# Linear attention followed by a gated convolution unit: another order of steps, other PSUM banks, and copies moved between engines

## The chip, the cores and the metric

The kernel runs on one core of a Trainium2 chip. The metric is the device time of one execution in microseconds (us), lower is better. Five engines work side by side, each through its own queue in order: TensorE (PE in the profile; its weight loads are PEld), VectorE (DVE), ScalarE (ACT), GpSimd (POOL) and SyncE (SP), which here only issues DMAs. GpSimd issues the loads of inputs in the same queue as its arithmetic.

## The reference

Inputs are float32. `q`, `k`, `v` have the shape (8 batches, 8 heads, 576 positions, 64), `w_phi` is 64 x 128, and the second part has two 512 x 512 weights and five taps for each of 512 channels.

```python
def phi(x):                                   # features of q and of k
    proj = x @ w_phi                          # [..., 576, 128]
    proj = proj - max(abs(proj), axis=-1)
    return concat([exp(proj), exp(-proj)])    # 256 features
kv  = sum over s of phi(k)[s, f] * v[s, d]
z   = sum over s of phi(k)[s, f]
att = (phi(q) @ kv) / (phi(q) @ z + 1e-6)     # [8, 8, 576, 64]
x   = att, heads side by side                 # [8, 576, 512]
gate = sigmoid(sum over t of conv_w[t] * x shifted down by 4 - t)
out  = (gate * (x @ w_val)) @ w_out           # [8, 576, 512]
```

## The kernel before

**Units and quads.** The 576 positions of a head are laid out as 128 partitions of nine half-blocks. The first eight half-blocks of a head make one unit; the ninth ones of the eight heads of two batches make another. So each of the four groups of two batches has nine units, 36 in all (numbers 0 to 35). Two heads form a quad (0 to 15), of which two make a batch (0 to 7).

**Tokens.** Everything that the kernel does is one of 1200 tokens in the string `ORDER`. A loop at the end of the kernel runs through them and calls the function of each, with its number, its PSUM banks (behind `@`) and its engine (behind `:`; `D` VectorE, `A` ScalarE, `P` GpSimd):

```python
    with tc.manual_schedule():
        for token in ORDER.split():
            head, _, eng = token.partition(":")
            head, _, bank = head.partition("@")
            ...
            ops[name](*args)
```

The order in the string is therefore the order of instructions in every engine's queue; no scheduler changes it. Waits between engines follow from the tiles that the instructions share. PSUM has eight banks of 128 x 512 float32, and the list names the bank of each product.

**The tokens that matter here,** with the number of their unit, quad, batch or output:
- `LK`, `LQ`, `LW`, `LC`: the first loads, on SP's and ScalarE's queues (LW the weights of phi, LC the five taps). `LD0` to `LD28`: the other loads, on GpSimd's queue (L331; LD27 is `w_val`, L336; LD28 is `w_out` in eight issues, L342).
- `CK`, `CQ`, `W2`: first casts of k, q and of the weights of phi (L254, L257, L260). `ND`: the negative identity (L251). `FL`: matmuls whose result nothing reads (L346).
- `T`: transposes of k and q of a unit on TensorE (L365, L370), `Tc` copies them out of PSUM (L245 on VectorE and GpSimd, L243 on ScalarE). From unit 24 on, but for unit 29, `TK` and `TQ` do this by a DMA transpose on SP's queue (L376).
- `PK`, `PQA`: products with the weights of phi, positions on the partitions (L393). `mK`, `mKb`, `mQ`, `mQa`: maxima of absolute values on VectorE (L411). `K0` to `K3`: exponentials for k on ScalarE (L460). `E`: factors exp of the maxima (L454). `V`: v times these factors, in GpSimd's or VectorE's queue: one 128 x 1024 product (L495) and a small cast (L500).
- `PQ` (L549), `SH` (the maximum taken off by matmuls, L557), `Qa` and `Q` (L580, two exponentials each): features of q.
- `KVa`, `KVb`: phi(k) times v (L523); `CA`, `CB` copy the result out of PSUM into the tile KVS. `NUM` (L622): numerator and denominator, three for a quad; `XN` divides (L628, L631).
- `XP`: transpose of a quad's result into the tile XT, by TensorE (L645, copied by `XC`) up to number 15, by a DMA on SP's queue (L641) from 16 on. `XQ` and `XD`: the same for the ninth half-blocks (L654). `HL`: the halo, the last four columns copied to the front shifted by one position (L245).
- `GA`: the convolution of a batch as matmuls with diagonal matrices (L692), `TH` its tanh on ScalarE (L702). `VAa`, `VAb`: two matmuls each of `x @ w_val` (L707). `GV`: gate times value on VectorE (L723). `OUT`: the output product, four matmuls (L732), `OE` takes it out of PSUM with a factor 0.5 (L739 on ScalarE, L741 on VectorE), `ST` stores it by SP's queue, `SU` by ScalarE's. Tokens ending in `t` (`GAt`, `THt`, `GVt`, `OUTt`, `OEt`, `STt`) do this for the ninth half-blocks of a group.
- `TP`, `CW`, `DG`, `DH`: the taps transposed and spread into diagonal matrices. `WS`: `w_val` into its final order.

The engine of a copying token picks the instruction:

```python
    def copy(eng, dst, x):
        if eng == "A":
            nc.scalar.activation(dst, x, AF.Copy)
        else:
            engines[eng].tensor_copy(dst, x)
```

Tiles rotate: six T tiles, four VT tiles, four KVS tiles, three output tiles of two outputs each. A token that writes one waits until the readers of the tile that it replaces are done.

Of the kernel before, what the change touches and what calls it, by code (L numbers as in the profile page):

```python
# [39 lines left out]
FL20@6 PQA2@0,6 mQa2 mQ2 PQ1@4,3 mQ3 SH1 Qa1 T4@0 Tc4:D T5@1 Tc5:D FL21@2 PK4@4,2 mKb4 Q1 PQA4@5,0  # L40
mQa4 K04 K14 K24 PQ2@6,7 SH2 Qa2 mK4 E4 V4:P PQA5@1,3 mQa5 mQ4 TP0@5 T6@4 Tc6:D PQ3@1,6 PQA6@4,0
K34 CW0 mQ5 SH3 mQa6 mQ6 T7@2 Q2 Qa3 PK5@3,7 KVa0@5,4 KVb0 mKb5 LD10 Q3 Tc7:D CA0:D CB0:D PK6@0,6
mKb6 K05 K15 mK5 T8@1 Tc8:D PQ4@2,5 LD9 K25 NUM0@4 XN0 K06 DG0:P SH4 KVa1@3,1 KVb1 K35 DH0:P K16
Qa4 Q4 PK7@7,4 E5 K07 K17 mK6 E6 CA1:D CB1:A mKb7 PQA7@2,0 mQa7 mQ7 PK8@3,5 K08 NUM1@0 mKb8 NUM3@2
XN1 LD27 K27 K37 PQ5@1,0 NUM2@4 mK7 K18 SH5 XN3 mK8 XN2 V5:P PQA8@7,3 mQa8 K26 mQ8 K28 Qa5 NUM5@2
# [6 lines left out]
Q8 VAa0@0 VAb0 NUM10@6 K012 GV0 K311 K212 XQ2@0 K112 XN10 K312 mK12 PK13@4,7 K013 NUM7@1 K111
XD2:A K113 XP6@3 XC6:A mKb13 K213 XN7 NUM11@6 XN11 PQ9@2,0 SH9 Qa9 mK13 mK11 XP5@1 VAa1@3 VAb1
K313 XC5:D XP4@4 XC4:A E11 Q9 XP7@6 XC7:D XQ3@5 PQ10@1,2 XD3:D HL3:P PQA12@7,6 GV1 HL2:P mQa12
PQA11@5,4 mQa11 SH10 Qa10 mQ12 Q10 E12 T14@3 Tc14:D mQ11 OUT0@7 E13 OE0:D GA1@5,0 V11:P KVa4@3,2
KVb4 PK14@4,7 TH2 VAa7@5 LD15 VAb7 VAa4@6 mKb14 TH3 K014 PQ11@0,1 K114 VAb4 GV7 mK14 LD18 LD16
T15@5 SH11 GV4 PQA13@4,6 K214 Tc15:D CA4:A CB4:A K314 Qa11 Q11 mQa13 PQA14@3,7 NUM12@2 PQ12@5,4
# [6 lines left out]
E16 K316 Tc19:D ST1 K017 K117 K217 VAb9 K317 mK17 GA2@2,5 TH4 PQA18@7,1 LD25 TH5 mQa18 OUT2@4 mQ18
T20@7 Tc20:A OE2:D PQA19@2,1 mQa19 PQ16@3,5 SH16 E17 PQA17@6,4 KVa6@7,2 V15:P V16:P Qa16 Q16 GV9
KVb6 LD22 LD17 mQa17 mQ17 PK18@0,6 mKb18 K018 CA6:A V17:P K218 LD26 T21@3 Tc21:D mQ19 OUT5@4 CB6:D
VAa11@5 VAb11 K118 OE5:A mK18 LD24 PK19@7,3 mKb19 K318 K019 K219 KVa7@1,2 PK20@4,0 mKb20 KVb7 K020
CA7:D K319 GV11 VAa10@6 VAb10 NUM18@1 GV10 CB7:D K120 mK20 PQ17@5,3 SH17 XN18 K119 K220 Qa17
VAa8@6 VAb8 GV8 K320 Q17 OUT4@2 mK19 PQA20@5,4 mQa20 PK21@1,6 K021 mKb21 OE4:A ST5 K221 OUT6@0
OE6:A mQ20 NUM21@7 T22@3 NUM20@5 K321 XN21 Tc22:A PQ18@2,4 XN20 NUM19@0 XN19 SH18 Qa18 XQ6@5 E18  # L70
V18:P XD6:D NUM22@7 XN22 NUM23@6 XN23 PQ19@3,0 XP12@5 XC12:D ST3 T23@7 Tc23:D XP13@2 SH19 TK24
TQ24 TQ25 XC13:D Q18 HL6:D XP14@6 XC14:D XP15@5 XC15:D K121 XQ7@4 XD7:D HL7:P Qa19 Q19 OUT9@7 mK21
PK22@2,3 K022 mKb22 E19 K122 OUT7@6 TK25 OE7:A ST7 OE9:D GA3@0,4 E20 mK22 V19:P TH6 PQA21@7,6
mQa21 VAa13@2 VAb13 E21 mQ21 PQ20@7,1 GV13 SH20 PQA24@0,6 mQa24 TH7 K222 OUTt0@4 mQ24 OEt0:D
VAa12@0 K322 Qa20 Q20 PQA22@5,2 V20:P KVa8@3,6 V21:P KVb8 mQa22 mQ22 E22 V22:P PK23@7,4 mKb23
# [12 lines left out]
XN33 TK32 OUT13@4 K329 OE13:A NUM35@0 mKb30 XN35 XQ10@5 NUM34@7 XN34 K130 mK30 XD10:A K230
PQ27@6,4 SH27 Qa27 E29 V27:P K330 XP22 Q27 XP23 XP20 ST13 V28:P VAa19@5 VAb19 OUT15@0 TK33 mQ30
PK31@7,6 OE15:D V29:P VAa18@2 VAb18 mKb31 XQ11@1 K031 PQ28@3,0 TQ33 SH28 GV19 XD11:A ST15  # L90
KVa12@4,1 GV18 TQ34 K131 K231 Qa28 mK31 PQA29@5,2 K331 KVb12 mQa29 Q28 OUT16@7 CA12:D CB12:A
PK32@3,4 PQA31@5,6 K032 mQ29 mQa31 PQ29@0,2 OE16:A mQ31 TK34 TQ35 SH29 Qa29 Q29 NUM36@1 XN36 K132
OUT17@5 OE17:D mKb32 HL10:P OUT19@7 OE19:D HL11:P K232 GA5@0,5 K332 TH11 mK32 NUM37@2 XN37
# [6 lines left out]
PQA35@1,4 XP26 GAt2@2 K135 HL12:D OUT20@5 mKb35 NUM43@0 HL13:P mQa35 mQ35 THt2 mK35 PQ34@1,4 K235  # L100
K335 OE20:A ST21 E34 SH34 Qa34 E35 NUM42@7 GVt2 XN42 GA6@2,5 ST19 VAa25@7 XN43 VAa24@1 VAb25 TH13
V34:P TH12 GV25 XP28 VAa26@0 VAb26 NUM44@5 XN44 XP29 PQ35@6,2 KVa15@3,7 Q34 V35:P KVb15 CA15:A
SH35 OUT22@4 CB15:D XQ14@5 VAa27@3 VAb27 Qa35 Q35 NUM45@7 VAb24 GV26 XD14:D ST17 HL14:P NUM46@0
# [767 lines left out]
```

## Time and profile before

| | |
|---|---|
| median of 3 runs | 220.04 us (218.84 to 220.24) |
| the profiled execution's own time | 219.92 us |
| its span | 218.1 us |
| TensorE clock granted, mean | 0.988 |
| busy: TensorE, VectorE, ScalarE, GpSimd | 199.3, 184.3, 188.7, 113.4 us |
| HBM read and written | 30.48 MB and 9.44 MB |

The span is what the profile shows; the execution's own time has some 1.8 us more around it. Matmuls are pipelined, so a busy TensorE is not one at its peak. The profile's lines name the source line, the engine, the operation and the tiles (out<-in); in a timeline the first two numbers are the start in us and the time from the first start to the last end, and the bracket at the end tells for how long the engine stood idle just before and what ended that.

### The profile page before, as it was taken

The page shows a single profiled execution, that of the slowest core. Times are in us where ns is not written, and L with a number is a line of the kernel's source. Part 1 is how long each engine was busy: PE and PEld are TensorE (multiplying, and loading weights), DVE is VectorE, ACT ScalarE, POOL GpSimd, SP SyncE. Part 2 cuts the span into 40 slices and gives each one's busy share as a digit, 9 for nine tenths or more (in the row PEclk, how much of TensorE's full clock was granted, in tenths as well). Part 3 has the DMA queues.
Part 4 walks back from the last instruction along what each step waited for, and adds up shares of the span by engine and source line. Part 5 has one row for each costly group of instructions (what it writes and reads, how often), then busy time and mean ns, then how long its engine had stood idle before and what let it go on. Part 6 is the DMA issues. An engine that isn't in the chain of part 4 may idle for free.

```text
span 218.1 us, 9723 instructions
## 1 busy us (share of the span) xinstructions
PE 199.3 (91%) x4171; PEld 133.8 (61%) x4202; DVE 184.3 (84%) x369; ACT 188.7 (87%) x426; POOL 113.4 (52%) x141
## 2 busy tenths in 40 slices
...
GB/s 154 185 208 190 94 164 163 109 109 99 201 19 60 208 99 205 204 128 208 218 227 99 129 162 67 85 8 99 121 126 180 117 118 77 132 150 138 187 177 189
DMA packets 40116, 30.61 MB, mean 140 GB/s; under 512 B 22021, under 2 KB 35205, under 8 KB 40074
## 3 DMA queue, kind: packets, MB, share of 16 engines
...
q10 hardware_dynamic: 624, 0.98, 1.4%
q8 instruction: 32, 0.52, 1.0%
...
HBM read 30.48 MB, written 9.44 MB: 183 GB/s over the span
## 4 chain that ended last, share of the span: by engine, by line
PE 61%; DVE 16%; ACT 9%; DMA 5%; issue 4%; SPq 2%; ACTq 0%; DVEq 0%
PE PS L732 11%; PE PS L707 9%; PE PS L622 7%; PE PS L393 7%; PE PS L523 6%; PE PS L557 5%; DVE MK L411 4%; PE PS L692 4%; ACT KTIL L460 3%; ACT QTIL L580 3%; DVE MQ L411 3%; PE PS L365 3%; DVE XN L631 3%; PE PS L549 3%; DMA OS<-in_k_dram 2%
## 5 line engine op out<-in xcount | busy, mean ns | idle before, releaser
L495 POOL TENSOR_TENSOR VT<-vN,E 128x1024 bf16<-128x1024 bf16 x36 | 68.6, 1907 | 51.0 <-issue 22.3
L460 ACT ACTIVATE KTIL<-PS 128x512 bf16<-128x512 f32 x144 | 84.0, 666 | 2.7 <-PE PS L393 1.9
L580 ACT ACTIVATE QTIL<-PS 128x512 bf16<-128x512 f32 x144 | 79.4, 676 | 1.2 <-PE PS L557 0.8
L411 DVE TENSOR_REDUCE MK<-PS 128x4 f32<-128x512 f32 x72 | 48.2, 683 | 3.7 <-PE PS L393 3.1
L411 DVE TENSOR_REDUCE MQ<-PS 128x4 bf16<-128x512 f32 x72 | 46.9, 683 | 2.3 <-PE PS L393 2.2
L707 PE MATMUL PS<-XT,WVAL 128*128 128x512 bf16 x109 | 31.2, 380 | 1.1 <-issue 0.3
L393 PE MATMUL PS<-W,T 64*128 64x128 bf16 x576 | 28.1, 219 | 3.9 <-DVE MQ L411 0.8
L732 PE MATMUL PS<-WOUT,GV 128*128 128x512 bf16 x116 | 30.7, 380 | 0.7 <-issue 0.2
L631 DVE TENSOR_TENSOR XN<-PS,RCP 128x384 bf16<-128x384 f32 x48 | 26.8, 558 | 1.7
L622 PE MATMUL PS<-KVS,QTIL 128*128 128x65 bf16 (+1 forms) x640 | 26.9, 195 | 1.4 <-DVE MQ L411 1.4
L622 PEld LDWEIGHTS <-QTIL 128*128 128x128 bf16 (+1 forms) x640 | 23.2, 100 | 8.1 <-issue 2.8
L393 PEld LDWEIGHTS <-T 64*128 64x128 bf16 x576 | 17.5, 94 | 16.3 <-issue 9.9
L723 DVE SCALAR_TENSOR_TENSOR GV<-GATE,PS 128x512 bf16<-128x512 bf16 x32 | 21.4, 682 | 4.4 <-ACT GATE L702 3.4
L245 POOL COPY XT<-XT 128x504 bf16<-128x504 bf16 x11 | 6.6, 606 | 35.2 <-DVE XT L245 13.5
L523 PE MATMUL PS<-VT,KTIL 64*128 64x65 bf16 x1152 | 22.2, 192 | 0.5 <-DVE T L245 0.4
L557 PE MATMUL PS<-nident,MQ 128*128 128x128 bf16 x288 | 22.5, 222 | 0.0
L523 PEld LDWEIGHTS <-KTIL 64*128 64x128 bf16 x1152 | 20.6, 96 | 2.1 <-issue 1.0
L557 PEld LDWEIGHTS <-MQ 128*128 128x128 bf16 x288 | 16.8, 99 | 6.9 <-issue 5.9
L732 PEld LDWEIGHTS <-GV 128*128 128x128 bf16 x128 | 11.2, 98 | 11.0
L702 ACT ACTIVATE GATE<-PS 128x1024 bf16<-128x1024 f32 x16 | 15.7, 1024 | 2.2 <-PE PS L692 2.1
L707 PEld LDWEIGHTS <-WVAL 128*128 128x128 bf16 x128 | 10.6, 98 | 10.6 <-issue 1.2
L741 DVE TENSOR_SCALAR OS<-PS 128x512 f32<-128x512 f32 x16 | 11.0, 685 | 5.9 <-PE PS L732 5.8
...
## 6 DMA issues: line engine op xcount, KB each, us to landing
...
kN<-in_k_dram POOLq DMA_DIRECT2D x7, 576.0 KB, 9.0
qN<-in_q_dram POOLq DMA_DIRECT2D x7, 576.0 KB, 5.8
vN<-in_v_dram POOLq DMA_DIRECT2D x7, 576.0 KB, 8.6
...
vN<-in_v_dram POOLq DMA_DIRECT2D x2, 288.0 KB, 11.5
...
```

The costliest lines, as they stand in the source:

```text
L393: nc.tensor.matmul(PS[:, bank[rg], blk * P:(blk + 1) * P], u.T[r, i, blk, :], W2[r, :], start=True, stop=True,)
L411: nc.vector.tensor_reduce(dst, PS[:, bank, :].rearrange("p (b f) -> p b f", f=F), AX.X, ALU.max, apply_absolute_value=True,)
L460: nc.scalar.activation(u.KT[:, ft, rg, :, :].rearrange("p b f -> p (b f)"), PS[:, u.PK[rg], :], AF.Exp, scale=1.0 if ft == 0 else -1.0,)
L495: e.tensor_tensor(u.VT[:, :, :, 0:D], unit_cols(u, "v").unsqueeze(1).to_broadcast([P, 2, 8, D]), E.to_broadcast([P, 2, 8, D]), ALU.mult,)
L523: nc.tensor.matmul(PS[:, m.kv[h2], o:o + E1], u.KT[r, ft, c % 2, c // 2, :], u.VT[r, ft, c, :], start=(j == 0), stop=(j == NJ - 1),)
L557: nc.tensor.matmul(PS[:, u.PQ[rg], blk * P + r.start:blk * P + r.stop], u.MQ[r, rg, blk:blk + 1].to_broadcast([r.stop - r.start, P]), nide ...
L580: nc.scalar.activation(u.QT[:, ft, :, rg, :], PS[:, u.PQ[rg], :].rearrange("p (b t) -> p b t", t=64), AF.Exp, scale=1.0 if ft == 0 else -1.0,)
L622: nc.tensor.matmul(y, f, k, start=(ft == 0), stop=(ft == 1), skip_group_check=True)
L631: nc.vector.tensor_tensor(m.XN[:, 3 * s:3 * s + 3, :].rearrange("p a (x d) -> p (a x) d", d=D), nv[:, :, 0:D], RCP[:, :].unsqueeze(2).to_b ...
L707: nc.tensor.matmul(PS[:, m.val[jt], :], WVAL[:, dt, jt * P:(jt + 1) * P], planes(m, dt, 0), start=(dt == 0), stop=(dt == 3),)
L723: nc.vector.scalar_tensor_tensor(out=m.GV[:, jt, :], in0=m.GATE[jt // 2][:, jt % 2, :], scalar=1.0, in1=PS[:, m.val[jt], :], op0=ALU.add, ...
L732: nc.tensor.matmul(PS[:, bank[0], :], m.GV[:, jt, j * P:(j + 1) * P], WOUT[:, jt, :], start=(jt == 0), stop=(jt == 3),)
```

## The change

Only the string `ORDER` is replaced. Both strings have the same 1200 tokens apart from banks and engines; nearly every token has another place in the list, and most products have another bank. The engines of 56 copying tokens differ. Counted by kind:

| token | before | after |
|---|---|---|
| Tc | 21 D, 4 A | 23 D, 2 A |
| CA, CB | 17 D, 15 A | 19 D, 13 A |
| XC | 13 D, 3 A | 15 D, 1 A |
| XD | 11 D, 5 A | 13 D, 3 A |
| HL | 5 D, 11 P | 8 D, 8 P |
| V | 36 P | 34 P, 2 D (V34, V35) |
| OE | 16 D, 16 A | 12 D, 20 A |
| ND | D | A |

The parts of the diff to which the prediction refers (whole lines of the lists, start, middle and end):

```diff
 ORDER = """
-ID0 LK0 LQ0 LW0 LD2 CK0 FL0@0 FL1@0 FL2@0 FL3@0 FL4@0 LC0 FL5@0 FL6@0 LD0 LD3 LD1 LD6 LD4 ND0:D
-FL7@0 CQ0 FL8@0 LD7 LD5 T0@0 Tc0:A LD8 FL9@7 FL10@7 FL11@7 W20 PQA0@4,5 mQa0 PK0@0,3 mKb0 K00 K10
-T1@6 FL12@7 FL13@7 FL14@7 K20 K30 FL15@7 FL16@7 Tc1:D PK1@2,4 mQ0 T2@3 K01 K11 mKb1 mK0 E0 mK1
...
-E7 V6:P KVb2 WS0:P XQ1@7 XD1:D LD13 XP0@4 XP2@6 Q6 XC2:D XP3@0 XC3:D HL1:P E8 XC0:A XP1@1 CA2:A
-CB2:A XC1:D HL0:D T10@3 PK9@6,7 K09 GA0@0,4 mKb9 K19 Tc10:D K29 V7:P V8:P K39 LD19 PQA10@3,2 mK9
...
-XP18 V23:P XQ8@5 XD8:D V24:P K325 SH24 mKb26 K125 XQ9@1 XD9:D XP19 K126 mK25 Qa24 K226 mK26 GAt1@5
-PQA26@0,1 mQa26 THt1 GVt1 KVa10@4,2 KVb10 K326 XP16 HL9:D Q24 CA10:A PK27@0,3 E25 CB10:A V25:P
-mQ26 mKb27 HL8:D K027 K127 T29@5 Tc29:D K227 E26 mK27 E27 TQ30 OUT11@6 OE11:D K327 OUTt1@7 GA4@1,4
...
-XQ13@7 XD13:D OE21:D V32:P V33:P KVa14@5,0 KVb14 CA14:D CB14:D XP24 TK35 PK35@7,6 K035 XP27
...
-OE22:A VAa31@6 GV27 XN45 XN46 XP30 NUM47@2 VAa28@7 OUTt2@5 XN47 XP31 OUT23@3 VAa29@0 OEt2:A STt2
-GV24 OUT24@1 OE24:A OUT25@4 OE25:A XQ15@2 XD15:A OE23:A OUT27@5 OE27:D OUT26@1 OE26:D HL15:P
-GA7@4,2 ST25 VAb29 TH14 VAa30@1 GV29 VAb28 TH15 VAb31 GV28 VAb30 GAt3@3 THt3 GV31 GV30 OUT28@0
-ST23 OE28:D ST27 SU28 ST28 OUT31@6 OE31:A SU31 ST31 OUT29@1 GVt3 OE29:D SU29 ST29 OUTt3@3 OEt3:D
-STt3 OUT30@0 OE30:A SU30 ST30 SUt3
+ID0 LK0 LQ0 LW0 FL0@0 FL1@0 FL2@0 LD2 FL3@0 FL4@0 ND0:A FL5@0 FL6@0 FL7@0 FL8@0 CK0 LC0 TP0@4 W20
+CW0 LD0 LD1 LD3 LD4 CQ0 T0@5 LD7 Tc0:D LD6 FL9@1 FL10@1 LD5 FL11@1 PK0@3,1 K00 K10 PQA0@5,4 T1@6
+Tc1:A mQa0 mKb0 K20 FL12@0 FL13@0 FL14@0 FL15@0 FL16@0 PK1@6,5 K01 PQ0@0,7 mK0 K11 mQ0 SH0 Qa0 E0
...
+KVb2 XP0@4 XC0:A XP1@7 E7 XC1:D XQ1@6 E8 XD1:A CA2:A XQ0@3 XD0:D XP3@1 CB2:A XC3:D XP2@5 XC2:D
+HL1:D WS0:P PK9@4,7 HL0:D mKb9 LD13 T10@3 GA0@0,5 Tc10:D PQA10@2,3 K09 K19 LD28 mK9 VAa2@4 K29 K39
...
+V7:P E9 Q7 T12@0 Tc12:D PQ8@4,6 K210 SH8 Qa8 NUM7@1 XN7 NUM8@3 XN8 KVa3@7,2 PK12@0,1 mKb12 V8:P
+KVb3 CA3:D PK11@4,3 K310 mKb11 Q8 CB3:D VAa3@5 VAb3 GV3 T13@7 Tc13:D K011 E10 LD16 K111 mK11 K012
...
+KVa9@3,1 K124 PK25@2,5 mKb25 TK28 KVb9 CA9:D K324 K025 K125 PQ23@4,7 SH23 Qa23 mK24 XP16 OUT12@0
...
+Q24 HL8:D K226 GAt1@0 THt1 E25 mQ25 XQ9@7 XD9:D V24:P OUT11@4 GVt1 K326 XP19 KVa10@3,6 KVb10
+CA10:D PK27@5,7 mKb27 HL9:P ST9 OUTt1@0 OE11:A K027 K127 E26 K227 K327 mK27 GA4@1,3 E27 TH8 CB10:D
...
+NUM42@0 XQ13@5 XD13:D PK35@2,6 mKb35 K035 K135 GAt2@3 HL13:P E34 HL12:D XN42 mK35 ST19 NUM43@7
+XN43 XP28 VAa26@1 THt2 GVt2 K235 K335 E35 PQ34@0,5 SH34 NUM44@2 XN44 GA6@6,3 VAa27@2 V34:D V35:D
...
+OUT24@6 OE24:A NUM47@4 XQ14@3 XN47 XP31 OE23:A ST23 OUT25@2 OUT27@5 OE27:D XD14:A HL14:P OUTt2@1
+OEt2:A XQ15@6 OUT26@0 VAa31@3 OE26:A XD15:D HL15:D VAa28@7 GA7@4,0 VAb31 TH15 TH14 OE25:D ST27
+GV31 VAb28 VAa29@6 VAb29 VAa30@2 VAb30 GV28 STt2 GV29 ST25 GV30 GAt3@0 THt3 GVt3 OUT28@2 OUT29@5
+OE28:A SU28 OUT31@4 ST28 OE29:D SU29 ST29 OE31:D SU31 ST31 OUT30@3 OE30:D SU30 ST30 OUTt3@0 OEt3:D
+SUt3 STt3
 """
```

In the list after, TK35 stands 76 tokens ahead of PK35.

More of the change, by code (lines that the diff above doesn't have):

```diff
@@ L40 @@
[L40 to L45, printed above, removed]
@@ L52 @@
[L52 to L57, printed above, removed]
@@ L64 @@
[L64 to L75, printed above, removed]
@@ L88 @@
[L88 to L93, printed above, removed]
@@ L100 @@
[L100 to L103, printed above, removed]
-OE22:A VAa31@6 GV27 XN45 XN46 XP30 NUM47@2 VAa28@7 OUTt2@5 XN47 XP31 OUT23@3 VAa29@0 OEt2:A STt2
-GV24 OUT24@1 OE24:A OUT25@4 OE25:A XQ15@2 XD15:A OE23:A OUT27@5 OE27:D OUT26@1 OE26:D HL15:P
```

83 lines of the change are left out of this document (57 added, 26 removed).

## The prediction

> **What bounds the kernel now.** I read the engine totals first, then the span cut into stretches, then the idle gaps in order of time. The cuts are the moments at which TensorE starts the eight gate convolutions, tokens GA0 to GA7 (L692).
>
> ```profile
> PE 199.3 (91%) x4171; PEld 133.8 (61%) x4202; DVE 184.3 (84%) x369; ACT 188.7 (87%) x426; POOL 113.4 (52%) x141
> ```
>
> No engine stands alone: three lie between 84 and 91%. Which of them sets the pace shows only by stretch (columns: start and end; length; busy time of PE, PEld, DVE, ACT, POOL with instruction counts; clock; DMA).
>
> ```profile
> 0.00:45.10 45.10, 36.37 (x668) 25.10 (x669) 36.69 (x74) 38.23 (x89) 33.43 (x52) 0.96 0.95 158
> 45.10:66.30 21.20, 19.57 (x407) 13.45 (x406) 19.96 (x42) 20.83 (x47) 16.82 (x22) 1.00 0.62 101
> 66.30:90.90 24.60, 24.32 (x571) 17.46 (x576) 22.41 (x46) 23.64 (x55) 13.14 (x17) 1.00 0.96 165
> 90.90:114.20 23.30, 23.04 (x506) 15.92 (x510) 22.51 (x49) 23.30 (x51) 12.13 (x14) 1.00 1.02 189
> 114.20:141.00 26.80, 26.33 (x624) 17.82 (x628) 24.83 (x49) 26.58 (x67) 13.46 (x13) 1.00 0.65 106
> 141.00:165.90 24.90, 23.50 (x485) 14.77 (x488) 24.08 (x47) 23.35 (x56) 10.33 (x12) 1.00 0.48 99
> 165.90:187.10 21.20, 20.79 (x518) 14.80 (x522) 19.84 (x41) 19.73 (x47) 8.82 (x10) 1.00 0.56 107
> 187.10:203.20 16.10, 15.94 (x268) 9.31 (x270) 8.16 (x19) 9.31 (x19) 5.28 (x6) 1.00 0.69 149
> 203.20:218.10 14.90, 9.43 (x165) 5.17 (x166) 5.84 (x9) 3.73 (x5) 0.00 (x0) 0.94 0.67 195
> ```
>
> Up to 187 us ScalarE and VectorE are both full to 91% or more (81% or more in the first stretch); from 187 us they idle for half of the time and TensorE is the bound. So a copy moved from ScalarE to VectorE before 187 us takes from one full queue and gives to another full one.
>
> **Prices.** An engine starts its next instruction before the last has ended, so the step between starts is the price, not the duration.
>
> ```profile
> 10.13 1.89 DVE L411 TENSOR_REDUCE MK<-PS 128x4 f32<-128x512 f32 x3
> 13.11 2.06 ACT L460 ACTIVATE KTIL<-PS 128x512 bf16<-128x512 f32 x4 [0.18 <-PE PS L393]
> 201.57 1.73 PE PS L732 x8
> 203.30 1.28 PE PS L692 x80
> ```
>
> Three reductions in 1.89 with 0.68 for the last: a step of 0.60 on VectorE. Four exponentials in 2.06 with about 0.62: 0.48 on ScalarE. Durations thus overlap by about 0.09 and 0.18 us, which I take off the other rows. An output product of four matmuls is 4 x 0.216 = 0.86 at most, one gate 1.28.
>
> ```profile
> L245 DVE COPY T<-PS 128x1024 bf16<-128x1024 bf16 x21 | 14.2, 682 | 0.3 <-PE PS L365 0.2
> L243 ACT ACTIVATE T<-PS 128x1024 bf16<-128x1024 bf16 x4 | 4.3, 1068 | 0.7 <-PE PS L365 0.7
> L245 DVE CAST KVS<-PS 128x260 bf16<-128x260 f32 x17 | 6.9, 423 | 1.0 <-PE PS L523 0.7
> L243 ACT ACTIVATE KVS<-PS 128x260 bf16<-128x260 f32 x15 | 6.5, 463 | 1.5 <-PE PS L523 1.5
> L741 DVE TENSOR_SCALAR OS<-PS 128x512 f32<-128x512 f32 x16 | 11.0, 685 | 5.9 <-PE PS L732 5.8
> L739 ACT ACTIVATE OS<-PS 128x512 f32<-128x512 f32 x16 | 10.7, 666 | 5.0 <-PE PS L732 3.3 <-DVE GVt L795 1.7
> L495 POOL TENSOR_TENSOR VT<-vN,E 128x1024 bf16<-128x1024 bf16 x36 | 68.6, 1907 | 51.0 <-issue 22.3 <-ACT E L454 11.5 <-PE PS L645 10.1
> L631 DVE TENSOR_TENSOR XN<-PS,RCP 128x384 bf16<-128x384 f32 x48 | 26.8, 558 | 1.7
> L245 DVE COPY XT<-XT x5: 284/381/1328, 45.4 to 182.9; 128x504 bf16<-128x504 bf16 x5
> ```
>
> **What moves.** The same 1200 tokens are in both lists. Net, VectorE gains 2 T copies (0.60), 2 KVS (0.34), 2 XC (0.33), 2 XD (0.13), 3 HL (0.25) and 2 V, and loses 4 OE (0.60) and ND (0.14). V on VectorE has no row: the slope from 384 to 512 elements is (683 - 558) / 128 = 0.98 ns, so 1024 cost some 1.18, a step of 1.1, and 0.2 for the small copy: 1.3. The ends are 0.7 (the T row, also 1024) and 2.1 (the POOL row and its 0.2); both V lie behind GA6, where VectorE has 8 of 16 us free, so neither end moves the sum. The Trainium skill has a rule against such moves ("Perfetto Trace Analysis", Optimizing Scalar/DVE Operations): reading PSUM costs VectorE some 125 ns of access, ScalarE 51. By it the eight PSUM copies gained less the four OE lost would cost 4 x 0.07 = 0.3 us more than their rows; the rows differ from it, as the T copy takes 682 ns on VectorE and 1068 on ScalarE, and the sum stays with the rows. The moves make +3.6 us on VectorE, -1.6 on ScalarE (4 OE more; 2 T, 2 KVS, 2 XC, 2 XD less) and -5.7 on GpSimd, which was never the bound.
>
> The other forms are priced in the same way, and TensorE's tokens by the step from one's first weight load to the next one's, the lower quartile of each kind. The tokens that each list puts between two marks, times their steps, are the queue work (us, before > after):
>
> | stretch | ACT | DVE | PE | longest |
> |---|---|---|---|---|
> | to GA0 | 35.6 > 35.1 | 35.9 > 36.8 | 27.7 > 27.7 | +0.9 |
> | GA0-GA1 | 20.9 > 21.0 | 20.8 > 19.2 | 16.4 > 16.2 | +0.1 |
> | GA1-GA2 | 22.4 > 22.0 | 21.5 > 21.3 | 21.8 > 22.0 | -0.4 |
> | GA2-GA3 | 22.6 > 22.2 | 22.0 > 23.7 | 21.4 > 21.6 | +1.1 |
> | GA3-GA4 | 25.9 > 25.2 | 24.7 > 24.6 | 23.8 > 23.6 | -0.7 |
> | GA4-GA5 | 22.6 > 23.6 | 22.3 > 23.2 | 20.6 > 20.6 | +1.0 |
> | GA5-GA6 | 18.8 > 17.4 | 19.2 > 19.5 | 18.9 > 19.8 | +0.6 |
> | GA6-GA7 | 7.4 > 8.7 | 7.5 > 8.0 | 14.3 > 13.2 | -1.1 |
> | from GA7 | - | - | 8.8 > 9.0 | +0.2 |
>
> The longest queue of each stretch grows by 1.7 us in all. Next the waits that the lists place.
>
> **Start, +0.5.**
>
> ```profile
> 5.56 0.40 PE L365 MATMUL PS<-ident_bf,kN 128*128 128x128 bf16 x4 [0.50 <-DVE kN L254]
> 6.21 1.02 ACT L243 ACTIVATE T<-PS 128x1024 bf16<-128x1024 bf16 x1 [0.70 <-PE PS L365]
> 6.64 0.52 DVE L260 CAST W<-wtmp 128x128 bf16<-128x128 f32 x1 [1.00 <-DMA wtmp<-in_w_phi_dram]
> 7.95 3.24 ACT L460 ACTIVATE KTIL<-PS 128x512 bf16<-128x512 f32 x6 [0.71 <-PE PS L393]
> ```
>
> The first T copy ran on ScalarE beside the wait for the weights of phi. Now it is on VectorE behind W2 and CW, so it runs from 7.25 to 7.93, against an end at 7.23; PK0 comes first after it instead of second, and the first exponential starts near 8.45 instead of 7.95. TP0, now ahead of T0 in TensorE's queue, is hidden by the same wait, as W2 cannot end before 7.16; without that cover its 0.4 us would count too. The ends are 0 and 0.7.
>
> **GA4, -1.4, and TK35, -0.4.**
>
> ```profile
> 139.82 1.90 POOL L495 TENSOR_TENSOR VT<-vN,E 128x1024 bf16<-128x1024 bf16 x1 [7.31 <-issue]
> 140.54 1.33 DVE L245 COPY XT<-XT 128x504 bf16<-128x504 bf16 x1
> 142.52 1.26 PE L692 MATMUL PS<-XT,DIAG 32*32 32x512 bf16 x68 [1.09 <-DVE T L245]
> 182.34 0.45 PEld L393 LDWEIGHTS <-T 64*128 64x128 bf16 x16 [0.32 <-DMA T<-kN]
> ```
>
> GA4 waits 1.09 us inside its matmuls and some 0.3 before them, 1.4 in all: its last transpose, XP16, was issued last of four on SP's queue, so the halo copy HL8 came late, met a V on GpSimd and took 1.33 instead of 0.28. The new list issues XP16 ahead of XP18 and XP19, 5 us of queue work before HL8. TK35 stood right before its reader PK35 (0.32 of wait and a little to restart); now it has 11 us. What is late next at GA4 is HL9 on GpSimd behind V24, with PK27, four exponentials and OUTt1 to cover it.
>
> **GA7, +1.0.**
>
> ```profile
> DMA to landing us min/median/max: 2.4/3.6/5.2
> 203.23 1.05 PEld L692 LDWEIGHTS <-DIAG 32*32 32x32 bf16 x80 [0.42 <-issue]
> ```
>
> Between NUM47 and GA7 the old list has six output products and the first halves of two VA for TensorE; the new one has four (OUT25, OUT27, OUTt2, OUT26), XQ15 and two such halves, 4 x 0.86 + 0.4 = 3.8 us. The chain beside it is XN47 (0.9 with its reciprocal), the transpose XP31 (3.6, with the ends 2.4 and 5.2), HL15 (0.3) and 0.4 of hand-over: 5.2. A stall of 1.4 instead of 0.42; ends -0.2 and +2.6. GA7, TH14, TH15 and everything behind them wait for it.
>
> **End, -0.5.**
>
> ```profile
> 211.82 1.03 PE L732 MATMUL PS<-WOUT,GV 128*128 128x512 bf16 x4
> 214.15 0.79 ACTq L817 DMA_DIRECT2D out_dram<-OSt  x1
> ```
>
> The last store was issued 1.3 us after the last matmul ended at 212.85, behind an OE and a store on ScalarE. Now OUTt3 is last and its copy is on VectorE: 0.7, then the store.
>
> **Sum.** 1.7 + 0.5 - 1.4 - 0.4 + 1.0 - 0.5 = +0.9. The profiled execution itself took 219.92 (span 218.1, 1.8 around it), near the median of 220.04: 219.9 + 0.9 = 220.8. I forecast no change that can be told from none, leaning to slower. About 1% (2.2 us) is what a measurement of this kernel can tell from no change.
>
> **Rivals.** *The halo copies wait for GpSimd (slower, 224).* HL on VectorE goes from five to eight. Of the five one met a running V and lost 1.05 us (1.33 against 0.28), and VectorE is full. If half of the eight meet one, that is 4 x 1.05 less the 1.05 of before: +3.2, so 224.0. For it: it happened once already. Against: V fills only 68.6 of GpSimd's 218 us and some HL stand where GpSimd has nothing. It decides from three HL rows above 1 us. The Trainium skill speaks here, "SBUF — State Buffer", Who interferes with whom: a VectorE copy in its two-port mode and a GpSimd instruction take one shared port pair, and the second to start blocks for the whole of the first. By that rule any HL beside a V pays up to a V's length, so all eight could; the trace agrees where it can, as the 1.33 us row ended 0.15 us after the V at 139.82 had.
>
> *Two V come late behind the loads of w_out (slower, 223.3).*
>
> ```profile
> L342 POOL DMA_DIRECT2D WOUT<-in_moe_w_out_dram x8 | 4.3, 541 | 2.4 <-PE PS L393 2.4
> qN<-in_q_dram POOLq DMA_DIRECT2D x7, 576.0 KB, 5.8
> kN<-in_k_dram POOLq DMA_DIRECT2D x7, 576.0 KB, 9.0
> 38.88 2.92 POOL L245 COPY WVAL<-OS 128x512 bf16<-128x512 bf16 x9
> 52.84 1.33 PE L523 MATMUL PS<-VT,KTIL 64*128 64x65 bf16 x72
> ```
>
> LD28, eight issues with 2.4 of waiting, moves on GpSimd's queue ahead of V7 and V8, which KVa3 and KVb3 (the last row) read from 52.84 on, V8 from 53.4. WS0 (the row above) ended at 41.8 and may again. If LD13, the q load issued next, lands in its 5.8, near 47.6, and the last of the eight issues waits for it, V7 starts near 48.4 and V8, two V of 2.1 later, ends near 52.5: in time. If it takes 9.0 as the k loads do, V8 ends near 55.7, TensorE stands for some 2.3 us and the reductions and exponentials behind it too: 220.8 + 2.5 with what restarts behind it, 223.3. It decides from a V7 that starts after 49.3.
>
> *The work evens out across the marks (faster, 216.3).* Queues may run ahead over a mark. Then only the running counts matter: at GA6 the fuller queue has 168.3 (VectorE) instead of 168.8 (ScalarE), -0.5; TensorE has 22.3 left instead of 23.1, -0.8; with GA4, TK35 and the end that is -3.6, if the start and XP31 are absorbed: 216.3. For it: the waits it removes are in the trace. Against: with two queues above 91% little has been absorbed so far.
>
> **How the numbers follow.** Forecast 0.42, own range 218.5 to 223.3 from the ends above (0.28 of it within 1%, 0.10 slower, 0.04 faster); GpSimd lock 0.15, slower; late V 0.14 (0.13 slower, 0.01 same); evening out 0.29 (0.27 faster, 0.02 same). So faster 0.31, same 0.31, slower 0.38. The range takes in 216.3 and 224.0 with 1.8 us beyond either: 214.5 to 226.
>
> **What would show it.** Right: the first KTIL near 8.45; no wait above 0.5 at GA4 or PK35; 1 to 2 us of idle TensorE ahead of GA7 behind HL15; VectorE busy near 188, ScalarE near 187; the last store within 0.8 of the last matmul. Wrong: HL rows above 1 us, V7 after 49.3, a GA6 more than 2 us from 188, or new gaps above 1 us at tokens not named here.

## The result, and the profile after

| | before | after |
|---|---|---|
| median | 220.0 us (218.6 to 224.2) | 219.4 us (215.9 to 226.9) |
| the profiled execution, its span | 219.92, 218.1 us | 217.16, 215.2 us |
| ratio to before | | 0.989 [0.985, 0.992] |

By the ratio the new list is 1.1% faster, 2.5 us, where 0.9 us slower was forecast. The ratios here, with 95% intervals, leave out the executions that took over 1.5% longer than the fastest of their kernel, which are one of 19 before but eleven of 19 after. Over all 19 of each the means are 220.1 and 219.9 us: the new list spreads more widely, and its mean execution gains almost nothing.

The engine totals of after, then the same cuts of the span as before, from one GA to the next (columns: start and end; length; busy time of PE, PEld, DVE, ACT, POOL with instruction counts; clock; DMA):

```profile
PE 196.2 (91%) x4171; PEld 132.2 (61%) x4202; DVE 186.6 (87%) x379; ACT 186.8 (87%) x423; POOL 107.3 (50%) x134
```

```profile
0.00:44.26 44.26, 34.38 (x668) 23.87 (x668) 36.55 (x74) 38.11 (x91) 32.11 (x50) 1.00 0.94 156
44.26:63.84 19.58, 18.74 (x400) 12.85 (x402) 19.25 (x43) 19.16 (x43) 14.67 (x19) 1.00 0.92 147
63.84:89.55 25.71, 24.69 (x572) 17.78 (x572) 23.83 (x49) 24.78 (x57) 12.51 (x17) 1.00 0.77 122
89.55:112.88 23.33, 22.97 (x515) 16.28 (x520) 23.07 (x49) 22.15 (x49) 14.22 (x16) 1.00 1.21 193
112.88:140.05 27.17, 25.93 (x619) 17.69 (x621) 25.22 (x50) 26.25 (x64) 13.47 (x14) 1.00 0.67 102
140.05:163.48 23.43, 23.22 (x487) 14.91 (x491) 22.65 (x47) 23.24 (x55) 10.73 (x12) 1.00 0.74 133
163.48:185.56 22.08, 21.75 (x529) 15.16 (x530) 20.38 (x42) 20.91 (x50) 8.96 (x10) 1.00 0.58 124
185.56:200.37 14.81, 14.65 (x253) 8.30 (x253) 9.51 (x20) 9.06 (x18) 0.61 (x1) 1.00 0.49 106
200.37:215.20 14.83, 9.83 (x167) 5.35 (x168) 6.14 (x10) 3.13 (x4) 0.00 (x0) 0.91 0.71 200
```

VectorE is busier by 2.3 us and GpSimd less by 6.1, where +3.6 and -5.7 were forecast. The stretches beside the prediction's terms for them (us; f1_bstart is the experiment that has the first part of before and the rest of after):

| stretch | forecast | before | after | change | f1_bstart |
|---|---|---|---|---|---|
| to GA0 | +1.4 | 45.10 | 44.26 | -0.84 | 44.09 |
| GA0 to GA2 | -0.3 | 45.76 | 45.29 | -0.47 | 45.49 |
| GA2 to GA4 | +0.4 | 50.16 | 50.50 | +0.34 | 49.81 |
| GA4 to GA5 | -0.4 | 24.91 | 23.43 | -1.48 | 23.42 |
| GA5 to GA6 | +0.2 | 21.13 | 22.08 | +0.95 | 22.07 |
| GA6 to GA7 | -0.1 | 16.18 | 14.81 | -1.37 | 14.82 |
| GA7 to the end | -0.3 | 14.9 | 14.9 | 0.0 | 14.9 |

Behind GA0 most of such a table is firm: where two kernels have the same list, their stretches agree to some hundredths (GA2 to GA3 took 23.38 to 23.39 us in seven profiles of the old list, 23.34 in ten of eleven of the new). Two stretches of the new list are not. GA3 to GA4 took 27.17 in after but 26.46 or 26.47 in nine of the eleven, and GA5 to GA6 took 22.00 to 22.08 in four profiles, after among them, and 21.76 to 21.77 in four others; so 0.7 of the +0.34 and 0.3 of the +0.95 belong to the profiled execution. Ahead of GA0 the table is not firm either, as the experiments show. So the three large differences to the forecast are the first part (2.2 us), GA4 to GA5 (1.1) and GA6 to GA7 (1.3).

### The profile page after: what moved, and what is told of

The parts are those of the page before. It is cut to its first block, busy times and chain, and to the rows that moved or that the text cites. A ratio compares the mean times of both kernels' runs of the same rounds, so it can differ in the third digit from the quotient of the medians.

```text
span 215.2 us, 9709 instructions
## 1 busy us (share of the span) xinstructions
PE 196.2 (91%) x4171; PEld 132.2 (61%) x4202; DVE 186.6 (87%) x379; ACT 186.8 (87%) x423; POOL 107.3 (50%) x134
## 4 chain that ended last, share of the span: by engine, by line
PE 64%; DVE 21%; DMA 6%; ACT 4%; issue 3%; SPq 0%; DVEq 0%
PE PS L732 11%; PE PS L707 11%; PE PS L523 7%; PE PS L622 7%; DVE MK L411 7%; PE PS L393 7%; PE PS L557 6%; DMA T<-qN 4%; PE PS L549 3%; DVE MQ L411 3%; DVE T L245 3%; DVE XT L245 3%; DVE XN L631 2%; PE PS L365 2%; PE PS L692 2%
## 5 line engine op out<-in xcount | busy, mean ns | idle before, releaser
L495 POOL TENSOR_TENSOR VT<-vN,E 128x1024 bf16<-128x1024 bf16 x34 | 64.8, 1905 | 37.2 <-issue 23.2
L411 DVE TENSOR_REDUCE MK<-PS 128x4 f32<-128x512 f32 x72 | 48.4, 682 | 2.5 <-PE PS L393 1.8
L622 PE MATMUL PS<-KVS,QTIL 128*128 128x65 bf16 (+1 forms) x640 | 26.4, 195 | 0.6 <-DVE MK L411 0.4
L245 POOL COPY XT<-XT 128x504 bf16<-128x504 bf16 x8 | 4.8, 606 | 44.3 <-DVE XT L245 14.9
L523 PEld LDWEIGHTS <-KTIL 64*128 64x128 bf16 x1152 | 20.0, 95 | 2.8 <-issue 1.0
L557 PEld LDWEIGHTS <-MQ 128*128 128x128 bf16 x288 | 16.3, 98 | 8.0 <-issue 7.4
L245 DVE COPY T<-PS 128x1024 bf16<-128x1024 bf16 x23 | 15.5, 682 | 0.9 <-ACT KTIL L460 0.4
```

Of the source, the lines that this page charges most:

```text
L411: nc.vector.tensor_reduce(dst, PS[:, bank, :].rearrange("p (b f) -> p b f", f=F), AX.X, ALU.max, apply_absolute_value=True,)
L495: e.tensor_tensor(u.VT[:, :, :, 0:D], unit_cols(u, "v").unsqueeze(1).to_broadcast([P, 2, 8, D]), E.to_broadcast([P, 2, 8, D]), ALU.mult,)
L523: nc.tensor.matmul(PS[:, m.kv[h2], o:o + E1], u.KT[r, ft, c % 2, c // 2, :], u.VT[r, ft, c, :], start=(j == 0), stop=(j == NJ - 1),)
L557: nc.tensor.matmul(PS[:, u.PQ[rg], blk * P + r.start:blk * P + r.stop], u.MQ[r, rg, blk:blk + 1].to_broadcast([r.stop - r.start, P]), nide ...
L622: nc.tensor.matmul(y, f, k, start=(ft == 0), stop=(ft == 1), skip_group_check=True)
```

## Experiments: parts of the change alone

**Three cuts.** e1_start, e2_tail and e3_mid join the two lists at GA1 and GA5.

```diff
 e1_start: -list after from GA1 on      +list before from GA1 on
 e2_tail:  -list before from GA5 on     +list after from GA5 on
 e3_mid:   -list before, GA1 to GA5     +list after, GA1 to GA5
```

> The list after up to GA1, the list before from there on. Start theory (the gain is made ahead of GA1, where the trace after is 2.49 us ahead: 63.84 against 66.33): about 217.6, ratio 0.989, and GA1 near 64 in the profile. Wait theory (the gain is what the prediction counted, GA4, TK35 and the end, and the early lead is spent again, as 1.2 of the 2.5 us are by GA2): 219.5 to 220.5, ratio 0.997 to 1.002. If the lead is only a matter of the one profiled execution of before, in which the granted clock fell to 0.83 between 20 and 30 us: ratio 1.000 and GA1 of both near 64.5 in other profiles.

> The list before up to GA5, the list after from there on (V34 and V35 on VectorE, XP31 and HL15 in another place, the last OUT in another order). Start theory: from GA5 to the end the two traces differ by 0.45 us (52.17 against 51.72), so 219.6, ratio 0.998. Wait theory: TK35 and the end save 0.9 and the lighter queue before GA6 0.5 more: 218.6, ratio 0.994. The prediction's own terms for this part (+0.6 -0.4 -1.1 +1.0 +0.2 -0.5) come to -0.2: 219.8.

> The list before up to GA1, the list after from GA1 to GA5, the list before from GA5 on. Start theory: between these marks both traces take the same time (99.6 us), so ratio 1.000. Wait theory: the 1.4 us at GA4 are saved here and something else in this stretch costs as much; with the queue work of the prediction (-0.4 +1.1 -0.7 +1.0 -1.4 = -0.4) 219.6, ratio 0.998; if the wait is removed and nothing is given back, 218.6, ratio 0.994.

Measured: 225.8 us, ratio 1.027 [1.021, 1.032]; 221.3, 1.006 [1.003, 1.010]; 223.1, 1.012 [1.006, 1.018]. All slower, so no theory is borne out, and the seams, where two lists are joined, are to blame in part: in e1_start KVa3 to GA1 took 14.96 us against 11.94 in after, as PQA11 stood next to a product that still held its bank; behind the seam at GA5, GA5 to GAt2 took 19.14 in e2_tail and 18.78 in e3_mid against 16.97 before and 18.21 after. Later cuts were made where the two lists have done the same work but for one or two tokens, and products next to the cut got banks that had been free for longer.

**Letters alone, order alone.**

```diff
 e4_engines: list before   -its engine letters   +those of after
 e5_order:   list after    -its engine letters   +those of before
```

> The order and the banks before, with the 56 engine letters of after (the copies moved to VectorE and to ScalarE, V34 and V35 on VectorE). If the letters alone make the gain (ScalarE relieved by 1.6 us, GpSimd by 5.7): ratio 0.99 to 0.995. If the order makes it and letters only fit their own order: 1.00 to 1.02, as VectorE gets 3.6 us more in a queue that was not arranged for it. The prediction's reading, that both queues are equally full, gives +1 to +3.6 us: 221 to 223.6.

> The order and the banks of after with the engine letters of before (56 tokens differ from after). If the order alone makes the gain: ratio 0.985 to 0.995. If letters and order only fit each other, as the letters alone in the old order suggest (1.076): ratio 1.02 to 1.08. If relief of ScalarE and GpSimd by VectorE is a plain sum of queue work: +1.6 us on ScalarE over after, ratio 0.995 to 0.998.

Measured: 236.3 us, 1.076 [1.071, 1.082], and 245.5 us, 1.115 [1.109, 1.121]. Neither half has the gain; each list is fitted to its own letters. One cause in e5_order, from the timelines of GpSimd and TensorE: 

```profile
45.67 0.60 POOL L243 COPY XT<-XT 128x504 bf16<-128x504 bf16 x1 [6.50 <-DVE XT L243]
46.21 2.95 POOL L243 COPY WVAL<-OS 128x512 bf16<-128x512 bf16 x9
49.09 0.74 POOL L329 DMA_DIRECT2D qN<-in_q_dram  x1
55.07 0.42 PE L368 MATMUL PS<-ident_bf,qN 128*64 128x128 bf16 x4 [3.85 <-DMA qN<-in_q_dram]
```

The halo copy HL1, on GpSimd again, waits there 6.50 us for its input, and the load of q that is queued behind it is issued at 49.09 instead of 42.09, so TensorE stands for 3.85. A letter's price is what stands behind it in the queue, not the copy's duration.

## Experiments: the first part and the clock

```diff
 f1_bstart: -first 248 tokens of after (up to GA0)   +first 248 tokens of before
            +GA0@0,4 VAa2@6 PQ7@7,2 PK10@3,5 NUM6@4
```

> The list before for its first 248 tokens (up to GA0), the list after from there on; one token (GA0) lies on the other side of this cut in the two lists, and five products next to it get a bank that has been free for longer. Start theory (GA0 comes 0.84 us earlier by the new first part): this loses 0.8 us against after, about 218.0, ratio 0.992. Clock theory (the lead at GA0 is only that the granted clock fell to 0.83 in the profiled execution of before, and the two first parts are worth the same): ratio 0.986 to 0.989, as after. If the seam itself costs, KVa3 to GA1 takes more than the 11.94 us of after.

Measured: 217.0 us median, 0.990 [0.986, 0.994]. The interval takes in the start theory's 0.992 as well as the clock theory's 0.989, so the ratio does not decide. The profile does: with the old first part GA0 comes at 44.09, a little ahead of after, where the start theory had it 0.84 behind. In the old first part the granted clock makes this difference (windows of before, then of h4_tq24, which has the same first part and begins 0.37 us later):

```profile
21.70:25.10 3.40, 2.17 (x32) 1.38 (x30) 3.28 (x7) 3.40 (x10) 3.08 (x4) 1.00 0.93 151
25.10:28.50 3.40, 3.40 (x64) 3.01 (x62) 2.25 (x4) 2.46 (x5) 3.23 (x7) 0.50 0.27 19
28.50:31.90 3.40, 3.04 (x89) 2.42 (x84) 3.28 (x8) 3.09 (x7) 3.40 (x5) 1.00 1.17 199
```

```profile
25.10:28.50 3.40, 3.19 (x112) 2.78 (x112) 3.38 (x8) 3.19 (x8) 3.31 (x6) 1.00 0.25 21
```

For 3.4 us TensorE runs at half speed and does 64 matmuls instead of 112. From K00 to GA0 the old first part took 35.74 and 35.76 us in two profiles without such a window, 37.11 to 37.15 in the five with one at 25 us, and 36.45 to 36.48 in the three with one at 36 us. A window at 25 us costs 1.4 us, and the profile of before that the prediction rests on had one, while that of after had none. Which of the three happens goes with the place of the 3.4-us windows: TensorE first had its full clock 4.03 and 3.75 us ahead of K00 in the two profiles without a window, 2.92 to 3.35 ahead in the five, and 2.20 to 2.53 in the three.

The new first part is worse off in the profiles at hand. In those of after, e1_start, f3_btail, f8_b827, h2_hl15 and h3_v34 GA0 starts at 44.26, 47.03, 45.81, 45.75, 47.56 and 46.98, mean 46.2; in ten of the old one at 44.06 to 45.18, mean 44.7. Two views of the same tokens, after and then h2_hl15 (experiments' line numbers are two lower, as their list has fewer lines):

```profile
6.15 0.40 PE L365 MATMUL PS<-ident_bf,kN 128*128 128x128 bf16 x4
7.56 0.62 PE L393 MATMUL PS<-W,T 64*128 64x128 bf16 x16
```

```profile
6.53 0.61 PE L363 MATMUL PS<-ident_bf,kN 128*128 128x128 bf16 x4
8.78 1.04 PE L391 MATMUL PS<-W,T 64*128 64x128 bf16 x16
```

In three of the six (e1_start, h2_hl15, h3_v34) TensorE first gets its full clock at about 10 us, in the others and in all ten of the old part between 4.3 and 6.3; K00 then starts at 9.1 to 9.4 instead of 8.0 to 8.3. Without any window of half speed the new first part takes 0.5 us more from K00 to GA0 (36.26 against 35.75), and GA0 comes at 44.26 against 44.06 and 44.09.

```diff
 i1_fl: -T0@5 ... FL9@1 FL10@1 ... FL11@1     +FL9@1 FL10@1 FL11@1 ahead of TP0
 i2_t0: -TP0@4 W20 CW0 ... T0@5               +W20 ... T0@5 TP0@4 CW0
```

> The list after with FL9 to FL11 moved from behind T0 to ahead of TP0, where TensorE stands from 4.5 to about 5.8 us. Idle theory (the idle time there lets the clock rise one step of 3.4 us later in some executions): the clock is full by 6.3 us, K00 near 8.1, K01 2.5 us behind it, the slow executions of after (over 219) are gone and the median is near 217, ratio 0.987. Otherwise the clock rises near 10 us in about half of the executions again, K00 near 9.3 there, and the times spread from 216 to 224 as those of after.

> The list after with TP0 and CW0 behind T0, as the list before has it; T0 then starts near 5.5 instead of 6.2. Order theory (what TP0 puts off is T0, and with it the work that brings the clock up): clock full by 6.3 us, K00 7.9 to 8.2, median near 217. If the rest of the new first part is the cause (Tc0 on VectorE, PK0 ahead of PQA0, other casts first): as after, the clock at 10 us in about half of the executions.

Measured: 218.4 us, 0.989 [0.984, 0.994], and 219.1 us, 0.992 [0.988, 0.996]. Neither steadies the kernel. In the profile of i1_fl the clock was full at 5.0 us and then fell three times, at 8.4, 22.1 and 28.9; in that of i2_t0 it rose in time and fell at 19.4 for 6.8 us. So the idle time ahead of TP0 and the place of T0 are not the cause alone; what else in the new first part costs clock stays open. Chance is not ruled out for the three late rises: one window earlier, the full clock would have come at 6.4 to 7.0 us there, and the ten profiles of the old part, with theirs at 4.3 to 6.3, never met that place. Nor does the spread go with the first part alone, as f1_bstart and h1_hl3, which have the old one, took 216.1 to 224.0 and 215.9 to 224.0 us.

## Experiments: GA4

The prediction put GA4's wait on XP16, the DMA transpose issued last.

```diff
 e6_dma:  -XP18 ... XP19 ... XP16    +XP16 XP18 ... XP19
          -TQ35 ... TK35             +TK35 TQ35
 g1_tc29: -HL8:D ... T29@5 Tc29:D    +T29@5 Tc29:D HL8:D
 g2_hl8:  as e6_dma, and -HL9:D ... V25:P ... HL8:D   +HL8:D HL9:D ... V25:P
```

> The list before with two tokens moved: the DMA transpose XP16 ahead of XP18, and TK35 ahead of TQ35. No engine letter and no bank changes. The prediction's own terms: 1.4 us at GA4 and 0.4 at PK35, so 218.0 to 218.5, ratio 0.992 to 0.994. Evening-out theory: the 1.8 us of idle time of ScalarE at this point were followed by a stretch that ran its queue work without a gap, so most of the 1.4 is kept. Rival, that ScalarE and VectorE bound the stretch and the wait only moves: GA4 to GA5 near 23.5 but GA5 to GA6 longer by as much, ratio 0.998 to 1.000.

> The list before with one token moved: HL8, the halo copy, goes behind Tc29 instead of ahead of it on VectorE. GA4 writes banks 1, 2, 4 and 5, and T29 holds bank 5 until Tc29 has read it. Port theory (HL8 cannot end before the product of V25 on GpSimd ends, and everything behind it on VectorE waits too, Tc29 first): Tc29 ends at about 141.2 instead of 142.5, HL8 ends as before 0.15 us after the V product (141.9), GA4 takes about 1.9 us instead of 2.45, GA4 to GA5 24.4 instead of 24.91. DMA theory (HL8 is long because XP16 lands late): GA4 unchanged at 2.45 or more. In the time at most 0.5 us, ratio 0.998 to 1.000.

> As e6_dma (XP16 and TK35 issued earlier), and HL8 moved ahead of HL9 on VectorE, where no V runs on GpSimd. Port theory: HL8 takes 0.28 instead of 0.86, Tc29 ends near 140.3, GA4 runs without its wait (1.05 instead of 2.45), GA4 to GA5 near 23.5 instead of 24.91; with the 0.38 of PK35 the sum is -1.8, ratio 0.992. If ScalarE and VectorE bound the stretch anyway: GA4 to GA5 near 23.5, but given back by GA6, ratio 0.998 to 1.000.

Measured: 220.0 us, 1.003 [0.999, 1.006]; 219.8, 1.000 [0.996, 1.003]; 218.8, 0.995 [0.991, 0.999]. The timelines around GA4, of e6_dma, g1_tc29 and g2_hl8:

```profile
139.89 1.90 POOL L493 TENSOR_TENSOR VT<-vN,E 128x1024 bf16<-128x1024 bf16 x1 [7.31 <-issue]
141.08 0.86 DVE L243 COPY XT<-XT 128x504 bf16<-128x504 bf16 x1
142.59 1.26 PE L690 MATMUL PS<-XT,DIAG 32*32 32x512 bf16 x68 [1.08 <-DVE T L243]
```

```profile
139.13 1.90 POOL L493 TENSOR_TENSOR VT<-vN,E 128x1024 bf16<-128x1024 bf16 x1 [7.31 <-issue]
140.54 0.64 DVE L243 COPY XT<-XT 128x504 bf16<-128x504 bf16 x1
141.23 1.13 PE L690 MATMUL PS<-XT,DIAG 32*32 32x512 bf16 x64 [0.16 <-DVE XT L243]
```

```profile
138.21 0.29 DVE L243 COPY XT<-XT 128x504 bf16<-128x504 bf16 x1
140.06 0.68 DVE L243 COPY T<-PS 128x1024 bf16<-128x1024 bf16 x1
140.82 0.65 PE L690 MATMUL PS<-XT,DIAG 32*32 32x512 bf16 x31
```

With XP16 early, GA4 waits 1.08 us as before; GA4 to GA5 is 24.91 in both. The wait is for Tc29 (the row always said `DVE T`), which reads bank 5, and GA4 writes banks 4 and 5. Tc29 stands behind HL8 on VectorE, and HL8 is long because GpSimd is inside the product of V25: it ends 0.15 us after that product, wherever it began. With Tc29 in front (g1_tc29) the wait falls to 0.16 and GA4 to GA5 to 24.31; with HL8 where no V runs (g2_hl8) it is gone, 23.52. From GA4 to the last store issue g2_hl8 takes 71.39 us against 73.14: nothing of the 1.75 is given back. Three moved tokens of the old list so make up a gain of their own. In after Tc29 stands ahead of HL8, and GA4 runs without a gap:

```profile
140.05 1.35 PE L692 MATMUL PS<-XT,DIAG 32*32 32x512 bf16 x80
```

**The same lock at GA1.** A VectorE copy that cannot end before a GpSimd product is called locked here. In after HL3 meets V11 (VectorE, GpSimd and TensorE around GA1):

```profile
63.43 1.50 DVE L245 COPY XT<-XT 128x504 bf16<-128x504 bf16 x1
62.89 1.90 POOL L495 TENSOR_TENSOR VT<-vN,E 128x1024 bf16<-128x1024 bf16 x1
64.99 1.06 PE L692 MATMUL PS<-XT,DIAG 32*32 32x512 bf16 x56 [0.51 <-DVE XT L245]
```

```diff
 h1_hl3 (list of f1_bstart): -HL2:P XC7:D ... HL3:D ... V11:P    +HL2:P XC7:D HL3:P ... V11:P
```

> f1_bstart (first 248 tokens of before, the rest of after) with HL3 on GpSimd, ahead of V11, instead of on VectorE beside V11, where it took 1.50 us. Port theory: HL3 takes 0.6 on GpSimd and ends before GA1 needs it, GA1 takes 1.05 instead of 1.93, and VectorE gets 1.5 us back: 0.9 us less than f1_bstart, 215.7, ratio 0.986. If ScalarE, which lags at GA1 by 2 us, sets the pace there: GA1 is shorter but GA1 to GA2 longer by as much, ratio 0.990.

Measured: 0.989 [0.982, 0.996], no different from f1_bstart. GA1 took 1.22 us instead of 1.92, but GA1 to GA2 was 25.65 against 25.71, so the lock is hidden there. That it is ScalarE's lag that hides it was expected, but is not shown by itself.

## Experiments: the tail

```diff
 f4_atail: -last 75 tokens of before (behind OUT22)   +those of after, ten banks changed
 f3_btail: -last 75 tokens of after                    +those of before, five banks changed
 f8_b827:  -list after from GA4 on                     +list before from GA4 on, five banks changed
```

> The list before for its first 1125 tokens (up to OUT22 and XN45), the list after for the last 75, with ten banks chosen so that none has just been used. Chain theory (GA7 waits in both kernels for NUM47, XN47, XP31, HL15, a chain of 7.02 us before and 5.34 after): 1.4 to 1.7 us less, ratio 0.9925 to 0.994. The prediction's terms for this part (-1.1 of queue work, +1.0 of a new wait, +0.2, -0.5) come to -0.4: ratio 0.998.

> The list after for its first 1125 tokens, the list before for the last 75. Chain theory: NUM47 to GA7 takes 6.8 to 7.0 us again instead of 5.34, HL15 starts 3.6 to 3.9 us after XP31 was issued and runs on GpSimd, and the time is 1.4 to 1.7 us over after: ratio 0.995 to 0.996 against before. If the tail of after only pays with its whole list (as its tail behind the list of before paid nothing): within 0.5 us of after, 0.989 to 0.991.

> The list after for its first 827 tokens (up to GA4), the list before for the rest, two tokens on the other side, five banks changed. XP16 is early here, so the wait inside GA4 should be gone: GA4 to GA5 near 23.4 instead of 24.91. Chain theory with a gain of 1.4 to 1.7 us in the tail, which this list doesn't have: 2.5 - 1.5 = 1.0 us below before, ratio 0.995. Evening-out theory (gains ahead of GA4 and in GA4 stay until the end): ratio 0.992 to 0.994. If everything that is gained ahead is taken back at GA6 by the fuller queue: ratio 1.000.

Measured: 220.5 us, 1.003 [1.000, 1.005]; 219.4, 0.997 [0.994, 1.001]; 220.3, 1.002 [0.998, 1.005]. NUM47 to GA7 goes with the tail's list alone: 7.01 us in f3_btail and f8_b827 as in before, 5.28 in f4_atail, 5.34 in after. But the stretch ahead of it answers: GA6 to NUM47 was 11.33 in f4_atail (VectorE stood at GV27 until 195.07, and TensorE's OUT24 waited for GV24 behind it), 8.52 in f3_btail, 9.16 before, 9.47 after. GA6 to GA7 is then 16.6, 15.5, 16.2 and 14.8, so the new tail pays only behind its own list. f8_b827 also has the new first part (GA0 at 45.75) and a seam that keeps GA4 to GA5 at 24.55.

```diff
 h2_hl15: list after, -HL15:D          +HL15:P
 h3_v34:  list after, -V34:D V35:D     +V34:P V35:P
```

> The list after with HL15 on GpSimd again, 0.61 us instead of 0.29. If TensorE's own tokens between NUM47 and GA7 set GA7 (XP31 to GA7 is 3.60 us in three profiles of this order while the landing varies from 2.57 to 2.96): GA7 at most 0.1 us later, same as after. If the chain over HL15 sets it, as the prediction had it: NUM47 to GA7 5.65 instead of 5.34, 0.3 us slower than after.

> The list after with V34 and V35 on GpSimd again. On VectorE each took 1.33 us, where the prediction had 1.3, behind GA6 with VectorE half idle. The prediction's step (they lie beside other work on either engine): within 0.3 us of after. Rival: V35 is read by KVa15, which starts at 189.5 in after; on GpSimd V34 and V35 take 4.2 us from about 186.4 on and V35 ends near 190.6, so KVa15 and what is behind it on TensorE starts 1.1 us later: ratio 0.994 against before.

Measured: 218.8 us, 0.995 [0.991, 0.999], and 224.1 us from four executions (217.5 to 227.8), without a ratio. By their stretches both letters are worth nothing: NUM47 to GA7 5.34 and GA6 to NUM47 9.47 in both, as in after. The times are those of the first part: GA0 at 47.56 and 46.98, and in h3_v34 a second window of half speed at 170.9 us. V34 on VectorE took what was forecast for it, 1.3 us (product and small cast, after):

```profile
186.37 1.22 DVE L495 TENSOR_TENSOR VT<-vN,E 128x1024 bf16<-128x1024 bf16 x1
187.50 0.20 DVE L500 CAST VT<-E 128x16 bf16<-128x16 f32 x1
```

**The lowest median.**

```diff
 h4_tq24 (list of f1_bstart): -ST5 ... TQ24 ... TK24     +TQ24 ... TK24 ST5
```

> f1_bstart with the store ST5 behind the DMA transposes TQ24 and TK24 on SP's queue instead of ahead of them. In four profiles of this order PQA24 starts 2.38 us behind GA3, in two 3.17 and 3.83, because TQ24 had not landed. If its late issue behind ST5 is the reason: PQA24 at 2.38 and a narrower spread of the times, median near 216.5. If the load of q is the reason (TQ24's issue then just waits for it): no difference to f1_bstart, ratio 0.990.

Measured: 216.6 us median (216.2 to 216.9), 0.985 [0.980, 0.989]. With the old first part, the new rest and the store behind the transposes it is 3 us below before. Its four executions lie within 0.7 us, but those of f1_bstart, one moved store away, did not, so steadiness is not shown; nor is a gain over after, as the intervals overlap. PQA24 started 2.38 us behind GA3 as hoped; as it does so in eight of ten other profiles of this order without the edit, the edit's own share is not shown either.

## Why the prediction was wrong, step by step

**To GA0, +1.4: mis-sized, and outweighed.** At an undisturbed clock the new part brings GA0 only 0.2 us later (44.26 against 44.06 and 44.09). Over all profiles it is 1.5, near the forecast, but by luck: the clock, which is no term of the forecast, makes most of it. In the two profiles compared the window of half speed in before, 1.4 us, outweighed it. The prediction had the row with a clock of 0.83 from 20 to 30 us in its own windows' mean (0.96 to GA0) and did not ask what it cost or whether it returns. K00 itself came at 8.00, not 8.45: the weights of phi were there earlier (W2 at 5.64, not 6.64), CW was done at 6.45, and Tc0 started at 6.82, not 7.25. In the ten profiles of the old part W2 starts anywhere from 5.4 to 6.8, so this term rested on the arrival in one execution.

**GA4, -1.4: right in size, wrong in cause.** XP16 had nothing to do with it. The step read HL8's 1.33 us as a late transpose that also met a V, and passed over `DVE T`, the releaser that the row names. TK35, -0.4, was right: in e6_dma GA5 to GA6 is 20.76 instead of 21.13.

**GA4 to GA5, queue work +1.0: this step failed.** By the count of tokens VectorE and ScalarE got the longer queues, yet the stretch shortened by 1.48, the whole wait. The old list's queue without the wait (g2_hl8) takes 23.52 us, the new list's queue 23.43, so the +1.0 is worth nothing. GA2 to GA3, with +1.1 forecast, measured -0.05. What the table added up as the longest queue of each stretch is not added: GA1 comes 2.49 us earlier while ScalarE still has Qa10 and Q10 to do, and by GA2 1.2 of it is gone. GA5 to GA6 took +0.95 (+0.64 in four other profiles) where +0.6 and -0.4 were forecast; only here did the longer queue show. PK35 waits for no DMA any more.

**GA7, +1.0: this step failed.** No new wait arose. After (SP, VectorE and TensorE's loads):

```profile
195.39 2.56 SPq L641 DMA_TRANSPOSE XT<-XN  x2
199.60 0.29 DVE L245 COPY XT<-XT 128x504 bf16<-128x504 bf16 x1 [0.63 <-DMA XT<-XN]
200.36 1.05 PEld L692 LDWEIGHTS <-DIAG 32*32 32x32 bf16 x80 [0.42 <-issue]
```

The idle time ahead of GA7 is 0.42, the same as before. Two terms were mis-sized. HL15 started 2.84 us after XP31 was issued at 196.76 (2.6 to 3.2 in the other profiles of this order), where 3.6 was taken, the median over all transposes. And TensorE's tokens between the end of NUM47 and GA7 fill 4.2 us, not 3.8. That h2_hl15 slows nothing shows that TensorE's queue, not the chain over HL15, sets GA7. What remains of the step is the queue work, -1.1 forecast, -1.37 measured.

**End, -0.5: right, and spent.** The last matmul ends at 210.41 and the last stores follow 0.76 us later, instead of 1.30. But that matmul ends 10.05 us behind GA7 instead of 9.62, where +0.2 was forecast, and GA7 to the end is 14.9 in both.

```profile
209.38 1.03 PE L804 MATMUL PS<-WOUT,GVt 128*128 128x512 bf16 x4
211.17 0.53 ACTq L817 DMA_DIRECT2D out_dram<-OSt  x1
```

**The signs.** Three that were named as wrong or right spoke against the forecast: the first KTIL at 8.00 and not 8.45, GA6 2.4 us ahead of 188, and one HL row above 1 us.

**The rivals.** *Evening out across marks* comes nearest to what happened behind GA0: 2.1 us less there in after, 2.6 in f1_bstart. It forecast -3.6 with the start and XP31 absorbed; no run tests its mechanism alone. *The lock on HL* is real, but only HL3 passed 1 us in after and it is hidden. *Late V*: V7 started at 48.72 behind the loads, against 48.4 reckoned and 49.3 as the point of decision; in time.
